# K's parameters loaded and worked in two halves, table loads as steps of the order, two late tiles by way of a ring, and a new order of steps

## The chip, the cores and the metric

The kernel runs on one core of a Trainium2 chip. The core's engines run side by side, each through its own queue in program order: TensorE (PE, with its weight loads PEld), VectorE (DVE), ScalarE (ACT), GpSimd (POOL) and the queue of SyncE (SP), which issues nearly all DMAs. The metric is the device time of one execution in microseconds; lower is better. A span is the time from the first to the last instruction in the trace.

## The reference

The input u is 2048 x 640 (length by channels), nearly everything is bf16. Two branches read it and a gate mixes them:

```python
g  = sigmoid((u * gate_w).sum(-1))                      # one number a row
# branch a: a long convolution with a kernel K of a diagonal state space
dt = exp(log_dt); logdA = dt * (A_re + 1j*A_im); dB = dt * (B_re + 1j*B_im)
K  = einsum("dn,dnl,dn->dl", C_re + 1j*C_im, exp(logdA[:, :, None] * l), dB).real   # 640 x 2048, n = 128
a  = irfft(rfft(u, 4096) * rfft(K, 4096))[:2048] + u * Dskip
# branch b: a gated feed forward, F = 1728
b  = (gelu(u @ w_gate) * (u @ w_up)) @ w_down
out = g * a + (1 - g) * b
```

## The kernel before

**One order, written by hand.** The function builds a dictionary of small named steps; the text ORDER (lines 40 to 89) lists their names, and the loop at lines 829 to 834 issues them one after the other. The order in the text is the program order of every engine: an engine takes its own steps out of it in that order, and waits where a semaphore for data or for a buffer isn't there yet. A name is followed by `/0` to `/3` where the step opens one of the four PSUM tiles `PS` (each 128 x 2 x 512), and by `/A` or `/D` where a copy may be done by ACT or DVE.

**K's parameters.** `lp0` to `lp5` (line 265) load A_re, A_im, C_re, C_im, B_re, B_im as six pieces of 128 x 640 (160 KB each), lp0 on ACT's queue, the others on SP's. `t0` to `t5` (`turn`, line 297) bring the 128 states onto the partitions: ten matmuls of 128 x 64 each. From these, steps `dt`, `al`, `al2`, `th`, `c2`, `c3`, `v0` to `v18`, `mag`, `at` and `ph45` (lines 317 to 350 and 560) work out the decay, the angle, the size and the phase of every (state, channel) on 128 x 640 tiles, each in one instruction of DVE or ACT.

**Tables of K, by halves h of the channels (320 each).** K at a lag is a product of a coarse and a fine power. `tables(h)` fills two tables: exponentials on ACT (`xb`, `xa`, lines 447 to 461), then phases on DVE (`fb`, `fa`, lines 469 and 477, each ended by a quarter-turn copy `ph_q`, line 464), sines on ACT (`sb`, `sa`, lines 481 and 487), and products on DVE (`pb`, `pc`, `pa`, `ma`, lines 492 to 505). `ct` (lines 517 and 518) contracts them over the states on PE, `ek` unloads PSUM (two or four casts of 128 x 504), `kd` and `kt` regroup the result through DRAM into KTt. The tables of the second half overwrite those of the first after its seven `ct`.

**ACT's function tables** are loaded by five steps with places of their own: `tabE` (exponential and logarithm), `tabT` (sine and arctangent), `tabE2`, `tabT2`, `tabG` (gelu and tanh), lines 316, 548, 558 and 617.

**Feed forward.** `g` and `u` steps (line 376) are gate and up projections of 128 columns each, for both halves of the rows (`.0`, `.1`): ten matmuls of 128 x 512 a step. Weights come in pairs into two slots (`lw0` to `lw13`), x by DMA transposes (`x0.0` to `x4.1`). The results are cast out of PSUM (`eg`, `eu`) into H or, through a ring of three tiles, to DRAM (`sg`, `su` into Gd and Ud), and come back later (`rg`, `rl`); `ge` is the gelu on ACT, `hm` the product on DVE. The tile H1 lies over the table space, so it is free only after the second contraction. The four tiles LATE = 8 to 11 of the second half of the rows are worked last and go straight into H1: `dg` (line 425) the gelu from PSUM, `du` (line 433) the product.

**Convolution.** In the spectrum: u is folded (`ul`, `ur`, `uf`, `us`) and turned by constant matrices FM (`U`, line 693), K by KMa and KMb (`K`, line 706); DVE multiplies the pieces (`m`, `s`, `y`, lines 748 to 755), IM turns back (`I`, line 766), and `D` (line 781) adds the down projection, `Z` (lines 788 and 789) mixes both branches with the gate in PSUM; `o` scales and `st` stores. `eU`, `eK`, `eI` copy out of PSUM. Names carry channel half, block of 512 rows and piece; the products of block 3 of half 1 end with `y130` and `y131`, followed by I130, I131, Z130, D131 and Z131. FM, KMa, KMb and IM are constants of the program and are loaded whole by `lfm`, `lkm`, `lkm2`, `lim` on SP's queue (lines 599 to 605).

Of the kernel before, what the change touches and what calls it, by code (L numbers as in the profile page):

```python
# [11 lines left out]
ALU = mybir.AluOpType  # L12
# [6 lines left out]
TURN = 65536.0  # L19
# [14 lines left out]
VIA = ()  # L34
# [6 lines left out]
ldt leu2 lp3 one oa.0 idx sk ob.0 lp0 lpk tdt/0 t0/1 tabE dt al xb27.0 al2 xa4.0 xb14.0 xb17.0 xb4.0 xb8.0 xa1.0  # L41
xb23.0 lp2 lw0 lp1 x0.0 lp5 x3.0 lp4 x1.0 x2.0 t1/2 th fb1.0 fb0.0 x4.0 t5/3 t2/0 xb2.0 c2 t3/1 c3 v3 v2 xa11.0 xb6.0
xa10.0 xa14.0 t4/2 v0 v1 v4 xa5.0 xb29.0 xb11.0 xb25.0 v6 v5 v7 v8 v11 g0.0/0 xb10.0 xa3.0 v9 v10 eg0.0/D v12 g1.0/1
v13 eg1.0/D xa8.0 xb9.0 xb5.0 xb1.0 xa7.0 xb19.0 v14 v15 xa19.0 xa15.0 xa17.0 xb15.0 xb13.0 xa9.0 v16 xb31.0 xb7.0
xa16.0 xb21.0 xb3.0 xb12.0 tabT sb0.0 u0.0/3 x3.1 leu0 ul0 lw1 ur0 uf0.1 eu0.0/D u1.0/2 g2.0/0 uf0.0 v17 mag ma2.0
u2.0/1 eu2.0/A ma4.0 eg2.0/D v18 su0.0 lw2 fil.0 ma6.0 ma1.0 eu1.0/D ur1 ma0.0 ma3.0 u3.0/3 fb2.0 pb0.0 pc0.0 sb1.0
fb3.0 eu3.0/A pb1.0 pc1.0 su1.0 lsk ul1 g4.0/0 g3.0/2 lw3 eg4.0/A sb2.0 pb2.0 fb4.0 pc2.0 eg3.0/A at ph45 su3.0 su2.0
us0 u5.0/1 u4.0/3 g5.0/0 lw4 sb3.0 pb3.0 pc3.0 fb5.0 eu4.0/A eu5.0/A sb4.0 g7.0/2 g6.0/3 eg6.0/A eg5.0/A u6.0/1 sb5.0
eg7.0/A pb4.0 pc4.0 fa0.0 pb5.0 fa1.0 sa0.0 su5.0 eu6.0/A u8.0/3 u7.0/0 lgw su4.0 x1.1 x2.1 lu00 x0.1 lw5 g8.0/2 su6.0
sa1.0 eg8.0/A g9.0/1 fa2.0 pa0.0 sa2.0 eu7.0/A uf1.0 uf1.1 pa1.0 u9.0/2 eg9.0/A eu8.0/A eu9.0/A fa4.0 pa2.0 fa3.0  # L50
sa4.0 g11.0/0 eg11.0/A sa3.0 lw6 g12.0/1 eg12.0/A su8.0 su9.0 x4.1 us1 su7.0 pa4.0 fa6.0 leu1 ul2 sa6.0 pa3.0 fa5.0
g10.0/3 eg10.0/A sa5.0 pa6.0 ma5.0 pa5.0 u11.0/2 eu11.0/A u10.0/0 u12.0/1 ur2 eu10.0/A ct0.2/3 ct0.1/2 ct0.4/0
eu12.0/A ek0.4/A fb0.1 uf2.0 ek0.2/D uf2.1 ct0.0/1 ct0.6/3 ek0.6/D ek0.1/A ct0.3/0 ct0.5/2 ek0.3/D ek0.0/D ek0.5/D
ks.0 lw7 su10.0 su11.0 h.0/3 eg13.0/D ul3 su12.0 us2 ob.1 ur3 tabE2 xa11.1 xb11.1 xb3.1 xb21.1 xa17.1 xb19.1 xa9.1
xa15.1 xa16.1 eu13.0/D uf3.0 ma5.1 lw8 h.1/0 oa.1 xa7.1 xb23.1 g12.1/1 xa3.1 xa14.1 xa10.1 ma3.1 eg12.1/D xb5.1 xb27.1
xb1.1 xb17.1 xa19.1 xb14.1 xb10.1 xb13.1 xb4.1 xb7.1 xb31.1 xb25.1 xb9.1 xa8.1 xb6.1 xb12.1 xb2.1 xb8.1 xa4.1 xb29.1
xa1.1 xa5.1 xb15.1 tabT2 sb0.1 u12.1/2 eu12.1/D su13.0 eg13.1/D sg13.1 sg12.1 leu3 su12.1 uf3.1 ma2.1 u0.1/3 eu0.1/D
ma6.1 g0.1/1 g1.1/2 kd.0 lw9 eu13.1/A gl/3 gl1 ma4.1 fb1.1 ma1.1 eg0.1/D sg0.1 su0.1 lfm ma0.1 us3 sb1.1 u1.1/1 g2.1/0
lw10 su13.1 fb2.1 pb0.1 pc0.1 pb1.1 pc1.1 sb2.1 U000/3 eg2.1/A eU000/A fb4.1 pb2.1 pc2.1 eg1.1/A eu1.1/A fb3.1 fil.1
sb4.1 sg2.1 u2.1/0 sg1.1 eu2.1/A su1.1 lkm fa0.1 pb4.1 pc4.1 sb3.1 g3.1/3 U001/2 eU001/A u3.1/1 eg3.1/A u4.1/0 U003/2  # L60
# [24 lines left out]
st110 D111/2 Z111 o111/A U131/0 eU131/A D120/3 m1210 s1220 m1211 m1221 s1221 m1200 s1200 m1201 s1201 m1320 m1310 s1320
y120 y121 m1311 m1321 s1321 m1330 s1330 m1331 K133/1 K131/2 eK131/A s1331 eK133/A m1300 s1300 m1301 s1301 y131 I121/0
# [53 lines left out]
def kernel(  # L140
# [724 lines left out]
```

## Time and profile before

| | |
|---|---|
| median of 3 runs | 290.28 us (289.33 to 291.79) |
| profiled execution | 288.91 us |
| its span | 287.1 us |
| PE busy | 264.5 us (92%) |
| DVE busy | 261.8 us (91%) |
| ACT busy | 222.7 us (78%) |
| DMA | 46.94 MB, mean 163 GB/s |
| granted TensorE clock, mean | 0.988 |

The page of the profile gives busy times of each engine and a picture of the span in 40 slices. Windows give the same for stretches that one chooses. The view of waits lists for each engine what ended its idle time: engine and line that waited, then who was waited for, the sum in us, how often, the longest. In groups and timelines a row is: line of the kernel, engine, operation, what is written and read, shapes, count; the groups then show the busy time and the mean length in ns of one, the timelines begin with start and length in us. The length of one instruction includes some overlap with the next of its engine.

### The profile page before, as it was taken

How to read it: one execution, taken by the hardware profiler on the slowest of the kernel's cores; microseconds unless marked ns; L12 is line 12 of the kernel's file. 1: busy time of each engine (PE TensorE's matmuls, PEld its weight loads, DVE VectorE, ACT ScalarE, POOL GpSimd, SP SyncE). 2: the span in 40 equal slices, each digit the busy share in tenths (PEclk: the TensorE clock that was granted, in tenths of full speed). 3: DMA queues.
4: the chain of work that ended last, by engine and by line, in shares of the span. 5: the costliest groups of instructions: out<-in, count | busy, mean ns of one | idle time of the engine just before them, and what ended most of it. 6: DMA issues, size and time to landing. Idle time of an engine off the chain costs nothing.

```text
span 287.1 us, 4933 instructions
## 1 busy us (share of the span) xinstructions
PE 264.5 (92%) x1883; PEld 159.8 (56%) x1883; DVE 261.8 (91%) x336; ACT 222.7 (78%) x324; POOL 14.1 (5%) x23
## 2 busy tenths in 40 slices
PE   3899799999999699998799998999999999999974
PEld 1744344444754434444584455777777767777753
DVE  1689999999998898999999999999999999999960
ACT  4699999799899978999999988999856545313320
POOL 2202000030040000000010000000000000000000
PEclk9999999999999969999999999999999999999999
DMA  7992479979382897858948877782355000010001
GB/s 200 221 227 75 136 223 272 213 182 304 101 265 66 193 321 220 301 186 263 332 117 222 278 200 215 225 256 67 95 142 162 25 23 23 25 46 25 23 23 46
DMA packets 63148, 46.94 MB, mean 163 GB/s; under 512 B 23275, under 2 KB 53526, under 8 KB 62998
## 3 DMA queue, kind: packets, MB, share of 16 engines
q1 hardware_dynamic: 62166, 44.90, 55.4%
q0 software_dynamic: 384, 1.31, 1.6%
q10 hardware_dynamic: 576, 0.43, 0.5%
q8 instruction: 14, 0.23, 0.3%
q14 instruction: 8, 0.07, 0.1%
HBM read 29.39 MB, written 14.62 MB: 153 GB/s over the span
## 4 chain that ended last, share of the span: by engine, by line
PE 36%; DVE 32%; ACT 17%; DMA 8%; issue 4%; SPq 2%; POOL 0%; DVEq 0%; ACTq 0%
PE ps L376 15%; DVE work L751 8%; DVE work L752 8%; PE ps L781 7%; DVE work L748 5%; PE ps L693 4%; ACT tail L481 3%; DMA work<-PMd 3%; PE ps L766 2%; ACT work L381 2%; ACT tail L487 2%; PE ps L706 2%; DVE work L383 2%; PE ps L517 2%; DMA tail<-PMd 2%
## 5 line engine op out<-in xcount | busy, mean ns | idle before, releaser
L376 PE MATMUL ps<-xT,Wr 128*128 128x512 bf16 x540 | 122.1, 385 | 7.1 <-DVE work L383 3.2
L376 PEld LDWEIGHTS <-Wr 128*128 128x128 bf16 x540 | 53.3, 99 | 72.4 <-issue 12.5
L381 ACT CAST work<-ps 128x640 bf16<-128x640 f32 (+2 forms) x59 | 47.8, 842 | 14.2 <-PE ps L766 7.5
L387 ACT ACTIVATE Wr<-ps,gs 128x320 bf16<-128x320 f32 x29 | 13.7, 524 | 29.4 <-issue 16.4
L752 DVE TENSOR_TENSOR work<-work 128x2560 bf16<-128x2560 bf16 x24 | 35.8, 1490 | 0.7
L781 PE MATMUL ps<-xT,work 128*128 128x320 bf16 x224 | 31.7, 299 | 0.0
L781 PE MATMUL ps<-xT,H 128*128 128x320 bf16 x224 | 31.6, 299 | 0.0
L481 ACT ACTIVATE tail<-work 128x1920 bf16<-128x1920 int16 x14 | 25.7, 1854 | 1.8 <-DVE work L464 1.7
L781 PEld LDWEIGHTS <-H 128*128 128x128 bf16 x224 | 21.9, 98 | 8.5
L781 PEld LDWEIGHTS <-work 128*128 128x128 bf16 x224 | 21.9, 98 | 8.5
L505 DVE TENSOR_TENSOR work<-tail,work 128x1920 bf16<-128x1920 bf16 (+1 forms) x22 | 23.1, 1090 | 0.0
L487 ACT ACTIVATE tail<-work 128x960 bf16<-128x960 int16 (+1 forms) x24 | 20.8, 926 | 0.8 <-DVE work L505 0.8
L766 PE MATMUL ps<-work,tail 128*128 128x320 bf16 x128 | 19.5, 299 | 1.8 <-DVE work L754 1.8
L469 DVE SCALAR_TENSOR_TENSOR work<-tail 128x320 int32<-128x320 f32 x42 | 18.0, 483 | 0.9 <-ACT tail L487 0.5
L464 DVE TENSOR_SCALAR work<-work 128x960 int32<-128x960 int16 (+1 forms) x26 | 16.5, 634 | 1.3
L766 PEld LDWEIGHTS <-tail 128*128 128x128 bf16 x128 | 12.4, 98 | 7.4 <-issue 2.2
L693 PEld LDWEIGHTS <-early 128*128 128x128 bf16 x128 | 12.4, 98 | 7.1 <-DMA tail<-PMd 1.7
L706 PE MATMUL ps<-KTt,early 128*128 128x320 bf16 x80 | 15.0, 299 | 1.4 <-ACT early L387 1.2
L496 DVE TENSOR_TENSOR work<-tail,work 128x1920 bf16<-128x1920 bf16 x14 | 15.9, 1151 | 0.3 <-ACT tail L481 0.3
L383 DVE CAST work<-ps 128x1024 bf16<-128x1024 f32 (+2 forms) x11 | 12.4, 1146 | 2.6 <-PE ps L766 1.6
L457 ACT ACTIVATE work<-tail 128x320 bf16<-128x320 f32 x30 | 12.5, 454 | 1.4 <-DVE tail L319 1.4
L693 PE MATMUL ps<-work,early 128*128 128x320 bf16 x80 | 13.1, 299 | 0.0
(119 smaller groups left out, 405.6 us busy)
## 6 DMA issues: line engine op xcount, KB each, us to landing
Ud<-work SPq DMA_DIRECT2D x22, 256.0 KB
work<-Ud SPq DMA_DIRECT2D x22, 256.0 KB
Wr<-in_B_w_gate_dram SPq DMA_DIRECT2D x12, 320.0 KB
Wr<-in_B_w_up_dram SPq DMA_DIRECT2D x12, 320.0 KB
PMd<-early SPq DMA_DIRECT2D x4, 640.0 KB
Gd<-work SPq DMA_DIRECT2D x9, 256.0 KB
work<-Gd SPq DMA_DIRECT2D x9, 256.0 KB
out_dram<-Wr SPq DMA_DIRECT2D x14, 160.0 KB
```

Of the source, the lines that this page charges most:

```text
L376: P.matmul(t[:, x, :], lhsT=Wr[:, slot, kt, cols:cols + 128], rhs=xT[:, th, kt, 512 * x:512 * x + 512], start=(kt == 0), stop=(kt == 4))
L381: A.copy(out=out, in_=in_)
L383: V.tensor_copy(out=out, in_=in_)
L481: act(out=T, in_=low16(t)[:, :, :, ::2], func=ACT.Sin, scale=SIN_SCALE)
L487: act(out=o[:, r], in_=i[:, r], func=ACT.Sin, scale=SIN_SCALE)
L505: tt(out=B2[:, :, :, cols].rearrange("p r g x -> p g r x"), in0=Tv if hf == 0 else Tv[:, :, ::-1], in1=e, op=ALU.mult)
L693: P.matmul(t[:, r, 0:W2], lhsT=FM[:, e, r, 128 * m:128 * m + 128], rhs=pm[:, r, e], start=(e == 0), stop=(e == 1))
L706: P.matmul(t[:, r, 0:W2], lhsT=mat[:, r, 128 * m:128 * m + 128], rhs=KTt[:, q, d], start=(x == 0 and j != 1), stop=(x == len(seq) - 1), sk ...
L751: step(f"m{h}{c}{i}{part}", lambda ux=ux, kx=kx: tt(out=fl(t), in0=ux, in1=kx, op=ALU.mult))
L752: step(f"s{h}{c}{i}{part}", lambda dst=dst, op=op: tt(out=fl(dst), in0=fl(dst), in1=fl(t), op=op))
L766: P.matmul(t[:, r, 0:W2], lhsT=IM[:, m, r, 128 * e:128 * e + 128], rhs=Y[:, r, m], start=(m == 0), stop=(m == 3))
L781: P.matmul(t[:, x, 0:W2], lhsT=H[c // 2][:, ft, tk:tk + 128], rhs=at[f"Wd{h}"][:, ft], start=(ft == 0), stop=False)
```

## The change

- The six parameters come as twelve pieces of 64 partitions: `lp0.0` to `lp5.1`, all but lp0.0 on SP. Each turn is done for one half of the channels (`t0.0` to `t5.1`, five matmuls of 64 rows), and every step from `al` to `ph45` exists for each half on 128 x 320. `dt` stays whole.
- Words `tE`, `tT` and `tG` in ORDER load a function table at that place; there are nine of them instead of five loads. The first stands ahead of ACT's own two loads.
- The quarter-turn copy of the phases is a step of its own (`qa`, `qb`).
- FM, KMa, KMb and IM are laid out by pieces and loaded in 4, 4, 2 and 2 parts.
- VIA = (8, 9): of the four late tiles, two are worked in the ring, stored to Gd and loaded into H1 again (`sg8.1`, `sg9.1`, `rg8.1`, `rg9.1`).
- ORDER is new throughout, with some copies given to another engine. From ACT to DVE: eK000, eK012, eU002, eU003, eU013, eg1.1, eg3.0, ek0.1, ek0.4, ek1.1, ek1.2, eu13.1, eu2.1, o1300, o1301, o1311. From DVE to ACT: eI131, eK011, eK013, eU010, eg1.0, eg13.0, eg7.1, ek1.5, eu13.0.

The diff, cut to its core (of ORDER, its beginning and its end):

```diff
-VIA = ()
+VIA = (8, 9)
...
-ldt leu2 lp3 one oa.0 idx sk ob.0 lp0 lpk tdt/0 t0/1 tabE dt al xb27.0 al2 xa4.0 xb14.0 xb17.0 xb4.0 xb8.0 xa1.0
-xb23.0 lp2 lw0 lp1 x0.0 lp5 x3.0 lp4 x1.0 x2.0 t1/2 th fb1.0 fb0.0 x4.0 t5/3 t2/0 xb2.0 c2 t3/1 c3 v3 v2 xa11.0 xb6.0
...
-y130 I120/2 D121/1 eI120/A Z120 o120/A eI121/A D130/2 Z121 o121/D I130/3 I131/0 eI130/A Z130 eI131/D D131/1 Z131 st111
-st120 st121 o1300/A st1300 o1310/D o1301/A st1301 st1310 o1311/A st1311
+tE oa.0 ob.0 one idx lpk lp0.0 lp1.1 ldt tdt/0 t0.0/1 dt al.0 xa10.0 lp5.1 lp4.0 lp2.0 lp3.0 xb19.0 al2.0 xa5.0 xa11.0
+lw0 lp1.0 xb13.0 t3.0/2 c3.0 xa7.0 xb3.0 xa16.0 xb8.0 xa15.0 x1.0 lp5.0 t2.0/3 x0.0 lp2.1 x2.0 lp3.1 c2.0 xb29.0
+xb14.0 xb17.0 t1.0/0 th.0 fb0.0 fb1.0 xb15.0 t5.1/1 t4.0/2 t5.0/0 v2.0 v1.0 v0.0 v4.0 v3.0 v5.0 v6.0 v7.0 v8.0 qb1.0
+xb11.0 v11.0 lp0.1 x4.0 x3.0 lp4.1 t3.1/3 t2.1/2 xa1.0 c2.1 qb0.0 c3.1 v2.1 v3.1 ur0 t0.1/0 t1.1/2 ul0 v9.0 v10.0
+t4.1/3 v12.0 v13.0 tT sb0.0 sb1.0 v0.1 v1.1 mag.0 v4.1 v5.1 tE v6.1 v7.1 v14.0 v15.0 xb21.0 xb7.0 u0.0/1 eu0.0/D
...
+s1321 m1330 s1330 m1331 s1331 K131/3 K130/1 eK131/A eK130/A m1300 s1300 m1301 s1301 eI111/A D101/0 D110/3 Z110 st100
+D111/1 Z111 o111/A y130 y131 Z101 I120/2 D120/1 o101/A eI120/A Z120 st101 o120/A o110/A D121/0 I121/2 eI121/A D130/1
+Z121 I130/3 I131/2 eI130/A Z130 eI131/A D131/3 Z131 st110 o121/D st111 o1300/D o1301/D st120 st121 o1310/D o1311/D
+st1300 st1301 st1310 st1311
...
+    kinds = {"tE": "natural_log_exp_and_others", "tT": "trig_and_small", "tG": "gelu_apprx_tanh_and_others"}
...
-    for i in range(6):
-        step(f"lp{i}", lambda i=i: (A if i == 0 else S).dma_start(out=at["prm"][:, i],
-                                                                 in_=PRM[i].rearrange("(p j) n -> p (j n)", p=128)))
+    def load_p(i, h):
+        rows = PRM[i].rearrange("(p j) n -> p (j n)", p=128)
+        (A if i + h == 0 else S).dma_start(out=at["prm"][64 * h:64 * h + 64, i], in_=rows[64 * h:64 * h + 64])
...
-    def turn(i):
-        t = PS[bank[f"t{i}"]]
-        for h in range(2):
-            o = t[:, h, 0:W2].rearrange("p (g j w) -> p j w g", g=16, w=4)
-            for j in range(5):
-                P.matmul(o[:, j], lhsT=at["prm"][:, i, 128 * j:128 * j + 128], rhs=ident[:, 64 * h:64 * h + 64],
-                         start=True, stop=True)
+    def turn(i, h):
+        o = PS[bank[f"t{i}.{h}"]][:, 0, 0:W2].rearrange("p (g j w) -> p j w g", g=16, w=4)
+        q = slice(64 * h, 64 * h + 64)
+        for j in range(5):
+            P.matmul(o[:, j], lhsT=at["prm"][q, i, 128 * j:128 * j + 128], rhs=ident[q, q], start=True, stop=True)
...
-    step("al", lambda: tt(out=two(at["al"][:, 0]), in0=pv(0), in1=two(at["dtb"]), op=ALU.mult))
+    def params(h):
+        d = slice(W2 * h, W2 * h + W2)
+        dtb, al, th, mag, ph45 = at["dtb"][:, d], at["al"][:, :, d], at["th"][:, d], at["mag"][:, d], at["ph45"][:, d]
+        va, vb, vr, vi, sm = (at[x][:, d] for x in ("va", "vb", "vr", "vi", "sm"))
...
+        s_("al", lambda: tt(out=al[:, 0], in0=pv(0), in1=dtb, op=ALU.mult))
...
-                    step(f"dg{ft}", lambda j=j, ft=ft: act(out=halves(H[1][:, ft]), in_=PS[bank[j]][:], func=ACT.Gelu_apprx_tanh))
+                    dst = ring() if ft in VIA else H[1][:, ft]
+                    step(f"dg{ft}", lambda j=j, dst=dst: act(out=halves(dst), in_=PS[bank[j]][:], func=ACT.Gelu_apprx_tanh))
...
+                    if ft in VIA:
+                        step(f"sg{ft}.1", lambda dst=dst, ft=ft: S.dma_start(out=Gd[:, ft], in_=dst))
...
-        ph_q(t, 3)
...
+                step(f"qa{c}.{h}", lambda t=t: ph_q(t, 3))
...
-    step("lfm", lambda: S.dma_start(out=at["FM"], in_=FMd))
+    for m in range(4):
+        step(f"lfm{m}", lambda m=m: load_part("FM", FMd, m, 512))
...
+    for ft in VIA:
+        step(f"rg{ft}.1", lambda ft=ft: S.dma_start(out=H[1][:, ft], in_=Gd[:, ft]))
...
         for word in ORDER.split():
             name, _, how = word.partition("/")
+            if name in kinds:
+                A.preload_act_table_set(kinds[name])
+                continue
```

More of the change, by code (lines that the diff above doesn't have):

```diff
@@ L56 @@
[L56 to L60, printed above, removed]
@@ L340 @@
-    step("v9", lambda: act(out=va, in_=va, func=ACT.Ln))
-    step("v10", lambda: act(out=sm, in_=va, func=ACT.Exp, scale=0.5))
-    step("v11", lambda: ts(out=vb, in0=vr, scalar1=0.0, scalar2=2.0, op0=ALU.is_ge, op1=ALU.mult))
-    step("v12", lambda: stt(out=sm, in0=vb, scalar=-1.0, in1=sm, op0=ALU.add, op1=ALU.mult))
-    step("v13", lambda: tt(out=vb, in0=vr, in1=sm, op=ALU.add))
-    step("v14", lambda: act(out=va, in_=vb, func=ACT.Square))
-    step("v15", lambda: act(out=va, in_=va, func=ACT.Ln))
@@ L353 @@
+    for h in range(2):
+        params(h)
     step("idx", lambda: G.iota(back[:], pattern=[[512, 4], [-128, 2]], base=255, channel_multiplier=-1))
@@ L603 @@
     step("hz1", lambda: G.memset(H[1][64:128, 13], 0.0))
-    step("lkm2", lambda: S.dma_start(out=at["KMb"], in_=KMd[:, 4096:6144]))
-    step("lim", lambda: S.dma_start(out=at["IM"], in_=IMd))
+    for m in range(2):
+        step(f"lkb{m}", lambda m=m: load_part("KMb", KBd, m, 1024))
+    for e in range(2):
+        step(f"lim{e}", lambda e=e: load_part("IM", IMd, e, 1024))
     def gate_mm():
```

198 lines of the change are left out of this document (106 added, 92 removed).

## The prediction

> **What bounds the kernel now.** I read the page first (who is busy, and when), then the windows that split the span into stages, then the waits of DVE, then the timelines of both ends, and last the groups by shape, for prices.
>
> ```profile
> span 287.1 us, 4933 instructions
> PE 264.5 (92%) x1883; PEld 159.8 (56%) x1883; DVE 261.8 (91%) x336; ACT 222.7 (78%) x324; POOL 14.1 (5%) x23
> DVE  1689999999998898999999999999999999999960
> PE 36%; DVE 32%; ACT 17%; DMA 8%; issue 4%; SPq 2%; POOL 0%; DVEq 0%; ACTq 0%
> ```
>
> Two engines are over 90% busy, and the chain passes from one to the other, so no single share names the bound. The windows do (columns: PE, PEld, DVE, ACT, POOL busy, granted clock, DMA):
>
> ```profile
> 0.00:20.00 20.00, 13.74 (x89) 8.98 (x90) 10.99 (x20) 13.94 (x26) 3.96 (x11) 1.00 0.98 228
> 100.00:120.00 20.00, 18.58 (x79) 8.28 (x79) 18.99 (x32) 17.50 (x21) 0.00 (x0) 0.85 0.93 289
> 120.00:140.00 20.00, 18.38 (x95) 9.09 (x94) 19.43 (x34) 20.00 (x20) 0.00 (x0) 1.00 0.79 240
> 180.00:276.00 96.00, 94.36 (x691) 67.30 (x690) 94.28 (x80) 54.58 (x96) 0.00 (x0) 1.00 0.28 83
> 276.00:287.10 11.10, 7.22 (x52) 4.98 (x51) 2.39 (x5) 2.16 (x4) 0.00 (x0) 0.99 0.14 44
> ```
>
> DVE is short of full only in the first 20 us and in the last 11. Its waits say the same:
>
> ```profile
> DVE tail L319 <- PE ps L297: 5.0, 1, 5.0
> DVE Wr L389 <- PE ps L789: 4.0, 1, 4.0
> DVE tail L322 <- PE ps L297: 3.0, 1, 3.0
> DVE work L383 <- PE ps L766: 1.6, 1, 1.6
> DVE work L383 <- DMA Gd<-work: 0.9, 1, 0.9
> DVE early L367 <- DMA early<-in_A_u_dram,back: 0.9, 1, 0.9
> DVE work L339 <- ACT work L338: 0.8, 1, 0.8
> DVE work L469 <- ACT tail L487: 0.5, 1, 0.5
> DVE early L383 <- PE ps L518: 0.4, 1, 0.4
> ...
> ```
>
> L319 and L322 lie in the first 10 us, L389 and the L383 behind L766 in the last 11. What is left, the five in between, is 0.9 + 0.9 + 0.8 + 0.5 + 0.4 = 3.5 us; the rows below them are 0.3 or less each. So between 10 and 276 us DVE has nearly nothing to wait for: its end is its start plus its work. And the end of the kernel hangs on it:
>
> ```profile
> 275.28 0.82 DVE L754 TENSOR_TENSOR work<-work 128x1280 bf16<-128x1280 bf16 x1
> 276.15 2.33 PE L766 MATMUL ps<-work,tail 128*128 128x320 bf16 x16 [1.77 <-DVE work L754]
> 278.86 3.97 PE L781 MATMUL ps<-xT,work 128*128 128x320 bf16 x28
> 283.41 0.55 DVE L389 TENSOR_SCALAR Wr<-ps,gs 128x320 bf16<-128x320 f32 x1 [4.00 <-PE ps L789]
> ```
>
> After the last product (y130 here) come two inverses, one more down projection, scaling and store: 287.1 - 276.1 = 11 us. In the new order y131 is last, and behind it PE has the same I130, I131, Z130, D131, Z131; I keep the 11 us. So I ask of each edit what it does to DVE ahead of that product.
>
> **Copies that change engine.** I compared the engine letters of both orders. Gate and up copies go four each way (eg3.0, eg1.1, eu2.1, eu13.1 to DVE; eg1.0, eg7.1, eg13.0, eu13.0 to ACT), those of K's spectrum two each way: nothing. Of the unloads of the contraction, four go to DVE (ek0.1, ek0.4, ek1.1, ek1.2) and one leaves (ek1.5): three more, two casts each. Of U's spectrum three go (eU002, eU003, eU013) and one leaves (eU010): two more. The three outputs that go to DVE at the very end lie in its idle time there, and eI131 leaves it: nothing.
>
> ```profile
> L383 DVE CAST early<-ps 128x504 bf16<-128x504 f32 x9 | 5.6, 674 | 0.5 <-PE ps L518 0.4
> L383 DVE CAST work<-ps 128x640 bf16<-128x640 f32 x2 | 1.6, 824 | 1.6 <-PE ps L766 1.6
> L344 DVE TENSOR_TENSOR work<-work 128x640 f32<-128x640 f32 x1 | 0.8, 824 | 0.0
> L469 DVE SCALAR_TENSOR_TENSOR work<-tail 128x320 int32<-128x320 f32 x42 | 18.0, 483 | 0.9 <-ACT tail L487 0.5 <-ACT tail L481 0.3
> L320 DVE TENSOR_SCALAR tail<-tail 128x640 f32<-128x640 f32 x1 | 0.5, 493 | 0.0
> L477 DVE TENSOR_SCALAR work<-tail 128x320 int32<-128x320 f32 x32 | 8.5, 318 | 0.0
> ```
>
> Six casts of 5.6/9 = 0.62 us are 3.7 us, two of 1.6/2 = 0.8 are 1.6: together 5.3 us more on DVE, and as much less on ACT, which has room (222.7 of 287.1).
>
> **Parameters by halves.** The same elements in twice the instructions. Fourteen DVE operations of 640 columns become 28 of 320, three that only scale become six. In a row of such operations one starts 0.74 us after the other:
>
> ```profile
> 13.05 0.81 DVE L334 TENSOR_TENSOR work<-ps,early 128x640 f32<-128x640 f32 x1
> 13.79 0.81 DVE L333 TENSOR_TENSOR work<-ps,early 128x640 f32<-128x640 f32 x1
> ```
>
> Half of one is nearest to L469: 18.0/42 = 0.43 us in a row, 0.48 alone. A split costs 2 x 0.43 - 0.74 = 0.12 to 2 x 0.48 - 0.82 = 0.14 us, fourteen times 1.7 to 2.0; for the scaling ones 2 x 0.27 - 0.49 = 0.05, three times 0.15. I take 1.8. That the phase and its quarter-turn copy become two steps changes no instruction. DVE's sum is 5.3 + 1.8 = 7.1 us, 6.4 if the copies run into one another as closely as the 0.74 shows for 0.82; I take 6.7, between them.
>
> **The start.** SP issues the loads of the parameters one by one, between the transposes of x:
>
> ```profile
> 6.02 0.57 SPq L265 DMA_DIRECT2D early<-in_A_B_im_dram  x1
> 8.05 0.58 SPq L265 DMA_DIRECT2D early<-in_A_B_re_dram  x1
> 8.68 5.45 SPq L280 DMA_TRANSPOSE xT<-in_A_u_dram  x4
> DMA to landing us min/median/max: 4.2/4.3/4.5
> 8.11 5.81 PE L297 MATMUL ps<-picks,early 128*128 128x64 bf16 x50 [3.20 <-DMA early<-in_A_A_im_dram]
> 13.67 1.13 PE L376 MATMUL ps<-xT,Wr 128*128 128x512 bf16 x4
> ```
>
> Five loads on SP become eleven; at about 0.45 us each SP is done 6 x 0.45 = 2.7 us later, at 16 to 16.5 instead of 14.1, and the last issue is lp4.1. Landing takes 4.3 us, so t4.1 can't run before 20, and every gate matmul stands behind it on PE: gate work starts at about 20.5 instead of 13.67. DVE has the first half's chain to work on meanwhile. Counted from th.0 (whose load lp1.0 again follows a pair of weight loads, so again at 9.4 to 9.7), it has two phases, six products, v8, two quarter turns, v11, two products of the other half, v12 and v13. That is some 8 us by the 0.43 and 0.27 above, with about 0.5 of waiting for the squares (0.8 at L339 today, where they are twice as long), so it stands at v0.1 at about 18.3: 2 us ahead of t4.1. Bounds 0 (the halves land sooner than whole loads) and +2.5; I take +0.8, nearer to the lower end, since what lands is half the bytes of that row. On ACT's queue the table load now stands ahead of the loads of picks and A_re:
>
> ```profile
> 0.75 0.38 ACTq L265 DMA_DIRECT2D early<-in_A_A_re_dram  x1
> 1.64 1.28 ACT L316 ACT_TABLE_LOAD   x1 [1.64 <-PEq L849]
> 79.61 1.28 ACT L548 ACT_TABLE_LOAD   x1
> 80.90 0.47 ACT L447 ACTIVATE work<-tail 128x320 bf16<-128x320 f32 x1
> ```
>
> That may put al.0 off by up to 1.3 us; th.0 waits for its own load anyhow (the 3.0 us of L322 covers it), so nothing; without that cover 1.3.
>
> **Tables of ACT.** Five loads become nine: 4 x 1.28 = 5.1 us, and some ten half activations more at 0.1 each. ACT gives up about what DVE takes over, and ends near its old sum; it has 2.5 us idle between 100 and 120, none between 120 and 140. The next activation starts at 80.90, right at the load's end. The Trainium skill, ScalarE: Activation LUTs, section What ACT_TABLE_LOAD costs, counts 1283 ns and a drain of 1380 ns for every switch, and its section on table sets says to do all of one set before the next, which speaks against this edit; by it the four would be an estimated 10.6 us. The trace shows the 1283 ns and no drain.
>
> **The rest.** FM, KMa, KMb and IM come in 12 pieces instead of 4, and two late tiles go out and come back: 12 more issues on SP at no more than the 0.58 above, spread over 100 us. The ring tiles let four of the late gate matmuls run ahead of the second contraction, so PE, not DVE, gains there. The cover is that loads are issued ahead of their use; where it is gone, a load is late by one issue, 0.6 us. I put all this at 0, bounds -1 and +1.5.
>
> **The sum.** Of the 3.5 us of waits in between, the new order can at most take all; some come back elsewhere, since ACT has no idle left at 120 to 140. I take 2.8 off. 6.7 + 0.8 - 2.8 = +4.7: span 291.8. The profiled execution took 288.91 (1.8 beside its span), the median of the runs is 290.28; with the same 4.7 the median is 295.0. Own range of this case: 6.4 + 0 - 3.5 - 1 = +1.9 to 7.1 + 2.5 - 2.0 = +7.6, so 292.2 to 297.9.
>
> **Rivals.** *Halves start DVE earlier.* A half is half the bytes. If th.0's load lands 2.0 us earlier and t4.1's in time, the 3.0 of L322 falls to 1.0, all 3.5 go, and 287.1 + 6.4 - 2.0 - 3.5 = 288.0 in the span, 291.2 as a median: not slower by the bound below. Over 1% faster needs another 3.8 us, from L319's wait and the tail. For: the two longest waits stand exactly there. Against: the DMA engines have 0.98 of busy share in these 20 us, and lp1.0 is queued behind the weights. It decides from L322's wait below 1.5 us. Chance 0.30.
>
> *PE takes over.* Its gates start 6.8 us later, and its remaining work is the same; in 180 to 276 it is busy for 94.36 of 96 us. If its stalls of today stay (20 - 18.58 and 20 - 18.38 in two windows alone), it ends 6.8 later and makes DVE wait for banks besides: 287.1 + 6.8 + 2 = 295.9, a median of 299. Against: the ring tiles fill two of these stalls. Chance 0.17.
>
> *Switching of tables stalls ACT for as long again as the load row shows,* as the drain of the page named above would. Two of the four added loads fall among the second half's tables, and there, from 100 to 140 us, ACT is busy for 37.5 of 40, so 2 x 1.28 go to DVE's waits: 291.8 + 2.6 = 294.4, a median of 297.6. The row at 80.90 speaks against it. Chance 0.03.
>
> **The numbers.** A measurement of this kernel tells about 1% (2.9 us) from no change. Forecast 0.50: mostly above 293.2, 0.42 slower and 0.08 same. Early halves 0.30: 0.20 same, and 0.10 faster, which stands for a start or a tail that I misread. PE and tables 0.20, slower. Together faster 0.10, same 0.28, slower 0.62. The range reaches from 288, three below the early-halves case, to 299.5, just over PE's.
>
> **What would show it.** DVE's busy time 268 to 270 instead of 261.8 (the three outputs included); the casts of 128x504 on DVE up by six, of 128x640 without a factor three of U's; first gate matmul at 19 to 21; nine table loads of 1.28; the last product at 280 to 282 and 11 us behind it. It is wrong if DVE is not busier by 6 us, if its first 20 us hold clearly more than 11 us of work, or if less than 10 us follow the last product.

## The result

The kernel after takes 294.37 us (median of 4 runs, 293.3 to 294.68), the kernel before 290.76 us on the same chip (4 runs, 289.33 to 291.79): 3.6 us more. The recorded ratio is 1.0134, 95% interval 1.0104 to 1.0163 (the quotient of the two medians is 1.0124). The forecast was 295.0. The profiled execution took 294.4 us with a span of 292.4, 5.3 more than before. The execution of the kernel before that was profiled, 288.91 us, is faster than each of these four, so some 1.7 us of what the two traces show between the kernels is chance between executions. From the page of the kernel after:

```profile
span 292.4 us, 4995 instructions
PE 264.8 (91%) x1870; PEld 158.5 (54%) x1883; DVE 264.9 (91%) x363; ACT 223.9 (77%) x328; POOL 28.1 (10%) x23
DVE  1587999999999999979997999899999999999971
DVE 43%; PE 17%; issue 14%; DMA 12%; ACT 9%; SPq 3%; DVEq 0%; ACTq 0%
```

DVE is busier by 3.1 us, not by 6 to 8, and PE's share of the chain fell from 36% to 17%. To see where the time went I cut both spans at three events that both kernels have: the first matmul of the first contraction, the end of the second half's last table product, and the end of the last spectrum product. Windows of before, then of after (columns as in the prediction: length, then PE, PEld, DVE, ACT, POOL busy, granted clock, DMA):

```profile
0.00:74.65 74.65, 65.27 (x322) 31.86 (x323) 64.52 (x104) 66.72 (x89) 8.93 (x15) 1.00 0.78 200
74.65:141.78 67.13, 61.36 (x487) 32.78 (x487) 62.92 (x102) 63.16 (x88) 3.59 (x5) 0.95 0.76 227
141.78:276.10 134.32, 130.70 (x1023) 90.15 (x1022) 132.03 (x130) 90.62 (x145) 1.61 (x3) 1.00 0.41 121
276.10:287.10 11.00, 7.22 (x52) 4.98 (x51) 2.29 (x4) 2.16 (x4) 0.00 (x0) 0.99 0.15 45
```

```profile
0.00:80.54 80.54, 68.57 (x326) 32.42 (x333) 67.13 (x126) 71.39 (x102) 24.57 (x17) 1.00 0.73 196
80.54:146.33 65.79, 61.16 (x483) 32.35 (x490) 64.03 (x109) 63.37 (x83) 1.37 (x3) 1.00 0.80 230
146.33:281.56 135.23, 128.40 (x1014) 89.13 (x1014) 130.84 (x125) 87.80 (x143) 2.14 (x3) 1.00 0.43 123
281.56:292.40 10.84, 6.70 (x49) 4.59 (x47) 2.94 (x7) 1.38 (x2) 0.00 (x0) 1.00 0.15 46
```

| stage | length | DVE busy | DVE idle (length less busy) | ACT busy |
|---|---|---|---|---|
| 1, to the first contraction | +5.89 | +2.61 | 10.13 to 13.41, +3.28 | +4.67 |
| 2, to the last table product | -1.34 | +1.11 | 4.21 to 1.76, -2.45 | +0.21 |
| 3, to the last spectrum product | +0.91 | -1.19 | 2.29 to 4.39, +2.10 | -2.82 |
| behind it | -0.16 | | | |

The loss is in stage 1, and ACT's work grows there more than DVE's; which of them carries the stage is told further below. DVE's waits after:

```profile
DVE tail L340 <- ACT early L322: 5.3, 1, 5.3
DVE tail L343 <- PE ps L310: 4.3, 1, 4.3
DVE Wr L413 <- issue: 3.4, 1, 3.4
DVE H L710 <- DMA work<-Ud: 3.1, 4, 1.6
DVE work L407 <- PE ps L400: 2.2, 1, 2.2
DVE Wr L413 <- PE ps L817: 1.5, 1, 1.5
DVE work L495 <- ACT tail L505: 1.4, 1, 1.4
```

The first two and the L407 are the start (the angle of the first half, and the first cast of a projection), the two L413 the end. Of the five waits of before between 10 and 276 us only the one for the squares is left, with 0.5; in their place stand `hm` products that wait for their tile to come back through the ring (L710), and a phase that waits for sines (L495).

### The profile page after: what moved, and what is told of

It reads as the page before. It is cut to its first block, busy times and chain, and to the rows that moved or that the text cites. A ratio compares the mean times of both kernels' runs of the same rounds, so it can differ in the third digit from the quotient of the medians.

```text
span 292.4 us, 4995 instructions
## 1 busy us (share of the span) xinstructions
PE 264.8 (91%) x1870; PEld 158.5 (54%) x1883; DVE 264.9 (91%) x363; ACT 223.9 (77%) x328; POOL 28.1 (10%) x23
## 4 chain that ended last, share of the span: by engine, by line
DVE 43%; PE 17%; issue 14%; DMA 12%; ACT 9%; SPq 3%; DVEq 0%; ACTq 0%
PE ps L809 7%; DVE work L779 5%; DVE work L529 5%; DVE work L780 5%; DMA Wr<-in_B_w_gate_dram 4%; PE ps L794 4%; ACT work L405 3%; DVE work L776 3%; DVE work L495 3%; DMA work<-Ud 3%; DVE work L407 3%; PE ps L400 2%; DVE work L490 2%; DVE early L391 2%; DVE H L710 2%
## 5 line engine op out<-in xcount | busy, mean ns | idle before, releaser
L400 PE MATMUL ps<-xT,Wr 128*128 128x512 bf16 x527 | 120.2, 384 | 4.0 <-DMA Wr<-in_B_w_gate_dram 1.5
L411 ACT ACTIVATE Wr<-ps,gs 128x320 bf16<-128x320 f32 x26 | 12.1, 527 | 22.4 <-issue 15.5
L384 POOL DMA_INDIRECT early<-in_A_u_dram,back x8 | 22.8, 2851 | 53.0 <-DVE early L391 37.0
L495 DVE SCALAR_TENSOR_TENSOR work<-tail 128x320 int32<-128x320 f32 x42 | 18.0, 481 | 1.4 <-ACT tail L505 1.4
L721 PE MATMUL ps<-work,early 128*128 128x320 bf16 x80 | 13.9, 299 | 2.4 <-ACT work L405 0.8
L407 DVE CAST work<-ps 128x1024 bf16<-128x1024 f32 (+2 forms) x11 | 12.8, 1178 | 2.3 <-PE ps L400 2.2
```

Of the source, the lines that this page charges most:

```text
L384: G.indirect_dma_start(out=at["ur"][:, e, :], out_offset=None, in_=u2[:, :], in_offset=bass.IndirectOffsetOnAxis(ap=back[:, 2 * c + e:2 * ...
L400: P.matmul(t[:, x, :], lhsT=Wr[:, slot, kt, cols:cols + 128], rhs=xT[:, th, kt, 512 * x:512 * x + 512], start=(kt == 0), stop=(kt == 4))
L407: V.tensor_copy(out=out, in_=in_)
L495: stt(out=t[:, 0, x], in0=at["th"][:, d], scalar=float(A_OF[3 * c + x] + MID), in1=at["ph45"][:, d], op0=ALU.mult, op1=ALU.add)
L721: P.matmul(t[:, r, 0:W2], lhsT=FM[:, m, e, r], rhs=pm[:, r, e], start=(e == 0), stop=(e == 1))
```

## Experiments

All times are medians; each ratio is to the kernel before, run beside it on the same chip. Differences to the kernel after are taken between sessions, in which the median of the kernel before lay between 289.77 and 290.76 us, so a difference of 1 us is not clear by itself.

**The quarter turn.** The prediction costed its separate step at nothing. Two runs ask that: the step added to the kernel before, and taken from the kernel after.

```diff
-        ph_q(t, n)
+                step(f"qb{c}.{h}", lambda t=t, n=n: ph_q(t, n))
...
-... fb2.0 pb0.0 pc0.0 sb1.0
+... fb2.0 pb0.0 qb2.0 pc0.0 sb1.0
```

> The kernel before, with the quarter-turn copies as steps of their own, one DVE step behind their phase; nothing else is changed, no instruction added. Theory (the quarter turn, which the prediction costed at nothing, is what DVE gained): a DVE instruction that reads what the one right ahead of it wrote starts about 0.03 us after that one's end, one that doesn't starts about 0.08 before it; 19 of the 26 pairs are taken apart, 19 x 0.11 = 2.1 us, so about 288.7 instead of 290.8, and DVE's busy time falls by about 1.5. Rival (the placing of the copy costs nothing, and the work that DVE lacked after the change went elsewhere): no change within 0.5 us.

293.26 us, ratio 1.008 (1.0047 to 1.0113): slower by about 1%. DVE's busy time fell, from 261.8 to 260.7 (1.5 was said), but stage 2 grew by 2.9 us. Each sine on ACT now starts one DVE step later, and DVE waits for it in turn:

```profile
DVE work L471 <- ACT tail L487: 2.3, 1, 2.3
DVE work L471 <- ACT tail L481: 1.5, 2, 1.1
DVE work L496 <- ACT tail L481: 1.1, 4, 0.3
```

In the kernel before these three pairs of engines cost 0.5, 0.3 and 0.3. Neither the theory nor the rival held: the copy's place is worth DVE time, and it is also the place from which ACT is fed.

```diff
-                step(f"qa{c}.{h}", lambda t=t: ph_q(t, 3))
+        ph_q(t, 3)
...
-... pc3.0 fa0.0 qb5.0 qa0.0 pc4.0 ...
+... pc3.0 fa0.0 pc4.0 ...
```

> The kernel after, with every quarter-turn copy right behind its phase again, as before; nothing else. Theory (the 26 dependent pairs cost 0.11 us each): +2.5 to +2.9 us, about 297, with DVE's busy time up by about 2. Rival: no change within 0.5 us.

296.36 us, ratio 1.0196 (1.0155 to 1.0236), 2.0 us above the kernel after; the two intervals overlap a little. DVE's busy time is 267.1 instead of 264.9, and 1.73 of these 2.2 us stand in stage 1, which is 2.23 us longer with the same work on ACT (this run's row of it, against 67.13 of DVE and 71.39 of ACT in 80.54):

```profile
0.00:82.77 82.77, 69.07 (x332) 32.47 (x333) 68.86 (x127) 71.48 (x102) 14.31 (x17) 1.00 0.74 196
```

The theory holds in DVE's work; in the whole time it is short, 2.0 us for 2.5 to 2.9. In the order after, with room for the later sines, the separate step is worth 2.2 us of DVE.

**The copies.** Nine engine letters, moved alone in either direction.

```diff
-... ek0.4/A ... ek0.1/A ... eU003/A ... eU002/A ... ek1.5/D ... ek1.1/A ek1.2/A ... eU013/A ... eU010/D
+... ek0.4/D ... ek0.1/D ... eU003/D ... eU002/D ... ek1.5/A ... ek1.1/D ek1.2/D ... eU013/D ... eU010/A
```

> The kernel before, with nine letters of the kernel after and nothing else: ek0.1, ek0.4, ek1.1, ek1.2, eU002, eU003, eU013 to DVE, ek1.5 and eU010 to ACT. Theory (DVE's work carries the end): six more casts of 128x504 at 0.62 and two more of 128x640 at 0.8 are 5.3 us more of DVE and the time grows by 4 to 5.3 us, to 295 to 296. Rival (DVE waits for ACT in these stretches, where ACT has no idle time): what ACT is relieved of comes back as shorter waits, and the time grows by less than 2 us.

> The kernel after, with the same nine letters set back to those of before. Theory (DVE's work carries the end): 4 to 5.3 us less, 289 to 290. Rival (after the change ACT carries nine table loads and the half activations, and is full from 100 to 146 us): DVE waits there for ACT instead, and the time stays within 1 us of 294.4 or grows.

Before with the letters of after: 306.0 us, ratio 1.0545 (1.0489 to 1.0601). After with the letters of before: 302.55, ratio 1.0417 (1.0379 to 1.0455), 8.2 above the kernel after. Both are worse: the first by far more than theory or rival allowed, the second on the side of its rival, which had put no size to it. Stage 2 of both, in the same order:

```profile
74.61:155.83 81.22, 66.64 (x488) 35.80 (x488) 66.85 (x108) 60.93 (x83) 3.59 (x5) 0.89 0.63 193
```

```profile
80.35:149.10 68.75, 62.82 (x489) 32.91 (x490) 61.56 (x103) 66.61 (x89) 1.03 (x3) 0.98 0.76 220
```

In the first, DVE is busier by 3.9 us and idle for 14.4 us instead of 4.2. It stands for 3.0 us at an unload of the contraction and for 5.1 at a copy of K's spectrum, with all its later work behind it, and PE waits for DVE in turn (3.85 us in the contraction, 3.70 ahead of a projection). In the second DVE has 2.5 us less to do and is idle for 7.2 instead of 1.8: ACT is at 66.61 of 68.75. That makes 3.0 us of loss; the other 5.2 lie in stage 3 (140.45 against 135.23 us), where one of the unloads set back to ACT now stands behind two gelus and PE waits for it:

```profile
160.94 1.76 PE L734 MATMUL ps<-KTt,early 128*128 128x320 bf16 x6 [4.92 <-ACT tail L405]
```

So the letters are not a term by themselves. Two readings are left, and no run separates them. One is that the copies are the other half of the table loads: ACT takes loads, DVE takes copies, and either half alone loses. The other is that an order written for one assignment loses with any other, whatever the loads. Stage 3 of the kernel after holds no table load, so its 5.2 us speak for the second.

**The table loads.**

```diff
-sb3.1 g2.1/0 ...
+tG tT sb3.1 g2.1/0 ...
...
-... eU001/A sa2.1 ...
+... eU001/A tG tT sa2.1 ...
```

> The kernel after with four more loads of ACT's function tables, as two pairs in the second half's tables (gelu's and back, ahead of sb3.1 and ahead of sa2.1), 4 x 1.28 = 5.1 us of ACT between 110 and 140 us. The prediction put the four loads that the change adds at nothing, because ACT has room over the whole span. If that holds: +1 us at most. Rival (in this stretch ACT is busy for 37.6 of 40 us and DVE's products wait for its sines): the loads come through one for one, +4 to +5.1 us, 298.5 to 299.5. Second rival (each load holds ACT for as long again): +8 to +10 us, and a gap of over 1 us behind each load.

300.64 us, ratio 1.0337 (1.0283 to 1.039): 6.3 us above the kernel after, for 5.1 us of loads. In the profiled execution stage 2 takes 72.99 instead of 65.79 us, and stage 1 is the same within 0.1. "Nothing" was wrong for loads in this stretch; the first rival (4 to 5.1) is nearest. ACT's timeline shows no second stall behind a load, 108.89 + 2.57 = 111.46:

```profile
108.89 2.57 ACT L860 ACT_TABLE_LOAD   x2
111.47 1.90 ACT L511 ACTIVATE tail<-work 128x960 bf16<-128x960 int16 x2
```

That speaks, as in the prediction, against the drain of 1380 ns that the Trainium skill, ScalarE: Activation LUTs, section What ACT_TABLE_LOAD costs, counts with every switch. What may make them cost more than their length is told under the clock, below.

**Working by halves.** The parameters of the kernel before worked, not loaded, by halves in place.

```diff
-... tabE dt al xb27.0 al2 xa4.0 ...
+... tabE dt al.0 al.1 xb27.0 al2.0 al2.1 xa4.0 ...
```

> The kernel before with the parameters worked, but not loaded or turned, by halves at the same places: 17 operations of DVE and 9 of ACT on 128x640 become two each on 128x320. The prediction's term is +1.8 us of DVE work (14 x 0.12 to 0.14 and 3 x 0.05) and as much in the time, 292.1. Rival (a half step can start while the other half is still on the other engine, so waits between ACT and DVE shorten): 0. Third case (each half waits for the one before it, and ACT's nine splits delay its exponentials): +3 or more.

290.24 us, ratio 1.0004 (0.9985 to 1.0022): nothing, the number of the first rival. Its reason, shorter waits, is not seen: DVE is idle for 25.4 us of the span, against 25.3. DVE's busy time grew by 0.7 us (262.5). The kernel after shows why it isn't 1.8. Half products with nothing between them start 0.40 apart, not 0.43, and 2 x 0.40 - 0.74 = 0.06; fourteen of these are 0.8:

```profile
12.35 0.48 DVE L352 TENSOR_TENSOR work<-ps,early 128x320 f32<-128x320 f32 x1
12.75 0.48 DVE L351 TENSOR_TENSOR work<-ps,early 128x320 f32<-128x320 f32 x1
```

**The start.** Two tries at taking back stage 1's loss in the kernel after, and one at the wait for the angle alone, in the kernel before.

```diff
-... lp0.0 lp1.1 ldt tdt/0 t0.0/1 dt al.0 xa10.0 lp5.1 lp4.0 lp2.0 lp3.0 xb19.0 al2.0 xa5.0 xa11.0
+... lp0.0 lp1.0 ldt tdt/0 t0.0/1 dt al.0 xa10.0 lp2.0 lp3.0 lp4.0 lp5.0 xb19.0 al2.0 t1.0/0 th.0
...
+... u0.0/2 v13.0 mag.0 v14.0 v15.0 xb17.0 xb15.0 eu0.0/D t3.1/0 c3.1 t2.1/1 c2.1 t5.1/3 t4.1/0 v2.1 ...
```

> The kernel after with its first 40 us in another order, the same steps: all first halves of the parameters are loaded first, then the first weights and x, then the second halves; the phase step fb0 and the first sines come before the squares of the size; the first two projections stand ahead of most turns of the second half; the later phases fb2 and fb3 stand ahead of the first cast. Theory (the start is what the change loses: its first contraction comes 5.9 us later than before, 74.65 against 80.5 us, and DVE waits for 12.3 of the first 40 us): the waits of 4.3 us (angle) and 2.2 us (first cast) go, the first gate matmul comes at 14 to 16 us, and the time falls by 3 to 5 us, to 290 to 291. Rival (ACT, with its exponentials and table loads, or the load of u, is as late as before): DVE waits for ACT before 40 us instead and the time changes by less than 1.5 us.

311.35 us, ratio 1.0767 (1.0707 to 1.0827). The angle came at 6.11 us and the first gate matmul at 11.56, earlier than the theory's 14 to 16, and then PE and DVE ran dry, the first row on PE, the second on DVE:

```profile
33.16 11.11 PE L400 MATMUL ps<-xT,Wr 128*128 128x512 bf16 x43 [5.70 <-DMA Wr<-in_B_w_up_dram]
```

```profile
39.13 1.23 DVE L407 CAST H<-ps 128x1024 bf16<-128x1024 f32 x1 [8.35 <-PE ps L400]
```

The second weight pair stood on SP behind `ur0`, which waits until all turns have read the parameters that it overwrites. The next run puts the weights ahead of it (its edit against this run).

```diff
-... lp1.1 lp4.1 xa15.0 ... ur0 ul0 xb21.0 ... lw1 eu1.0/D u2.0/2
+... lp0.1 lp1.1 lw1 fb2.0 tE ... t1.1/2 ur0 ul0 al.1 th.1 ... eu1.0/D u2.0/1
```

> The start of the experiment before, mended where its trace shows the loss: the second weight pair is loaded ahead of ur0 and ul0 (those two wait on SP for the turns, and the weights stood behind them until 33 us), the turns of the second half run in one go behind the first projection, and ACT's two copies c3.1 and c2.1 stand ahead of its late exponentials. Theory (the start is what the change loses, and a microsecond gained by DVE ahead of the first contraction reaches the end): no wait of 8 us at 39, first contraction at 76 to 78 instead of 80.5, time 290 to 292. Rival (the first 80 us are bound by ACT, whose exponentials and sines are the same sum, 76.8 of the 80 us from 20 to 100 us being busy): DVE's early lead is lost in waits for ACT before the first contraction, and the time stays at 293 to 296.

303.7 us, ratio 1.0487 (1.043 to 1.0545). Neither the theory nor the rival: that wait is gone, and the next queue shows (DVE, then PE):

```profile
DVE early L391 <- DMA early<-in_A_u_dram,back: 6.1, 1, 6.1
```

```profile
45.77 14.60 PE L400 MATMUL ps<-xT,Wr 128*128 128x512 bf16 x56 [8.76 <-ACT H L405]
```

The first folds of u came 2.6 us later than in the kernel after (27.32 against 24.77), and the next one waits for its load. Both runs lose behind 20 us what they gain ahead of it; neither says what the kernel after's start would be worth if it could be had alone.

```diff
-ldt leu2 lp3 ... al2 xa4.0 ... lp2 lw0 lp1 x0.0 ... x2.0 t1/2 th fb1.0 fb0.0 ...
+ldt leu2 lp1 ... al2 t1/2 th fb1.0 fb0.0 xa4.0 ... lp2 lw0 lp3 x0.0 ...
```

> The kernel before with one pair of loads exchanged on SP, whole parameters as before: lp1 (the angle) is issued first and lp3 in its place, behind the first weights; its turn, the angle and the first two phases stand right behind al2, and ACT's copies c2 and c3 some exponentials earlier. It puts the wait of L322 by itself: 3.0 us before the change, 4.3 after it. Theory (DVE's end is its start plus its work): the angle comes at 6.4 to 6.6 instead of 9.39, the first cast at 17.8 instead of 19.6, and 1.5 to 3 us reach the end, 287.5 to 289. Rival (ACT, busy for 19.9 of the 20 us from 20 to 40, or PE's first projection sets the pace there): DVE waits for them instead, 0 to -0.5 us.

289.69 us, ratio 0.9979 (0.9955 to 1.0003): the rival. In its trace the angle stands 3.1 us earlier, the first contraction 0.43 us, the end nowhere:

```profile
6.30 0.81 DVE L322 SCALAR_TENSOR_TENSOR tail<-ps,early 128x640 f32<-128x640 f32 x1
11.90 0.82 DVE L334 TENSOR_TENSOR work<-ps,early 128x640 f32<-128x640 f32 x1 [1.86 <-ACT early L326]
19.42 1.22 DVE L383 CAST H<-ps 128x1024 bf16<-128x1024 f32 x1 [0.47 <-PE ps L376]
```

1.86 of it go at once to a wait for ACT's copy of C, 0.47 to PE's first projection. In the kernel before, a wait of DVE in the first 20 us is not paid one for one: ACT and PE set the pace there.

**The waits for the ring.**

```diff
-hm1.0 K000/3 ... rl4.0 ... eK000/D ks.1 ...
+K000/3 ... rl4.0 ... eK000/D ks.1 hm1.0 ...
...
-hm13.0 ... rl2.1 m0210
+... rl2.1 m0210 hm13.0
```

> The kernel after with two products of the feed forward moved: hm1.0, which waits 1.6 us for its tile from the ring, behind eK000 and ks.1; hm13.0, which waits 0.74, behind m0210. Theory (DVE's waits in the middle add to the end one for one): 1.5 to 2.3 us less, 292 to 293. Rival (PE, which is 93 to 100 per cent busy from 180 us on, ends no earlier, or the ring is freed later and the wait comes back at the next product): no change within 0.7 us.

306.94 us, ratio 1.0582 (1.0546 to 1.0617). This measures something else than it was meant to. `rl4.0` and `rl2.1` fill the same ring tiles as the two products that I moved behind them, so those products work on tiles 4 and 2, and must wait for them: DVE waits 14.7 us for two loads. The next run moves these loads too; in it, D000 of the down projection still reads tile 13 of H ahead of its product.

```diff
-hm1.0 ... rl4.0 ... ks.1
+... ks.1 hm1.0 rl4.0
...
-hm13.0 ... D000/2 ... rl2.1 m0210
+... D000/2 ... m0210 hm13.0 rl2.1
```

> The kernel after with hm1.0 behind eK000 and ks.1, and hm13.0 behind m0210, each with the one load that fills its ring tile next behind it (rl4.0, rl2.1), so that every product reads its own tile again. Theory (DVE's waits in the middle add to the end one for one): of 1.6 and 0.74 us of waiting 1.5 to 2.3 go, 292 to 293. Rival (PE is 93 to 100 per cent busy from 180 us on, or the loads moved back bring the wait again at hm4.0): no change within 0.7 us.

294.39 us, ratio 1.015 (1.01 to 1.0199): unchanged. Here the product must wait until D000 has read its tile, and what the other product had gained goes there:

```profile
184.95 0.68 DVE L710 TENSOR_TENSOR H<-H,work 64x1024 bf16<-64x1024 bf16 x1 [2.44 <-PE ps L809]
```

So one product alone:

```diff
-hm1.0 ... rl4.0 ... ks.1
+... ks.1 hm1.0 rl4.0
```

> The kernel after with the one product hm1.0, which waits 1.60 us for its tile, behind eK000 and ks.1, and the load rl4.0 that fills its tile next behind it. Theory (a wait of DVE in the middle adds to the end one for one): the first product of the spectrum starts 1.5 to 1.8 us earlier, as it did in the last experiment (158.33 against 160.14), and 1 to 1.8 us reach the end, 292.6 to 293.4. Rival (the lead of 1.8 us is lost behind 180 us, where PE is over 93 per cent busy and DVE waited 2.4 us for PE in that experiment): no change within 0.5 us.

293.25 us, ratio 1.0104 (1.0076 to 1.0133): 1.1 us less than the kernel after, as the theory has it at its lower end, though the intervals overlap. In the trace stage 3 is shorter by 0.84 us, and the waits for the ring fell from 3.1 to 2.2 us:

```profile
146.20:280.59 134.39, 128.56 (x1014) 89.20 (x1014) 130.82 (x126) 87.70 (x143) 2.14 (x3) 1.00 0.43 123
```

The way of the two late tiles through the ring was not undone by itself, but the trace of the kernel after shows what it does to the loads. SP stores the two tiles (L460), and the next load into the ring (L709) stands for 2.6 us until such a store has landed; the load that `hm1.0` waits for is issued 1.0 us behind it, at 153.56 (SP's timeline, then its waits from 146 to 156 us):

```profile
148.09 1.45 SPq L460 DMA_DIRECT2D Gd<-work  x2
152.56 0.32 SPq L709 DMA_DIRECT2D work<-Ud  x1
```

```profile
SPq L709 <- DMA Gd<-work: 2.6, 1, 2.6
```

No version beat both kernels; the fastest, the earlier angle, can't be told from the kernel before.

## Why the prediction was right, and where it was not

**The form of the sum** held. The last product ends at 281.56 (280 to 282 was said), 10.84 us follow it (11), the first gate matmul starts at 19.14 (19 to 21), there are nine table loads of 1.28, and the first 20 us hold 9.71 us of DVE's work (at most 11). Up to the last product the sum was 6.7 + 0.8 - 2.8 = 4.7; measured, in the stages above, it is 2.53 of work + 3.28 of start - 0.35 of other waits = 5.46. Two large errors of opposite sign made a good total; that is luck. The medians moved by 3.6 us for the 4.7 that was forecast.

**DVE's work, 6.7: measured 2.53**, and by the prediction's own line ("wrong if DVE is not busier by 6 us") its account of the work was wrong, though the time came out. Three steps of it failed. "Changes no instruction", of the quarter turn: worth 2.2 us of DVE. Halves at 1.8: 0.7. Copies at 5.3: 5.0 by the letters added to the kernel before (261.8 to 266.7), 3.3 by those taken from the kernel after (264.9 to 261.6). With 3.3 to 5.0, 0.7 and -2.2 the sum is 1.8 to 3.5, and the 2.53 lies in it.

**Copies as a cost and table loads at nothing** was a further error. The prediction read ACT's room from the whole span (222.7 of 287.1). By stage there is next to none: 66.72 of 74.65 us and 63.16 of 67.13. It named the full stretch from 100 to 140 itself, and used it only for a rival at 0.03. Four further loads in that stretch cost 6.3 us for 5.1, and the copies, set back, cost 8.2 us where the prediction's term has a gain. That the copies pay for the loads is one reading of this; the runs do not show it. The rival *switching of tables* was wrong in its mechanism (no drain), right in where it looked.

**The start, 0.8: measured 3.28 of DVE's idle time.** The wait that it priced, for t4.1 not before 20 us, did not come: lp4.1 was issued at 15.38 (the working's 14.1 + 2.7 would put SP's end at 16.8, not 16 to 16.5), its turn ran at 18.50, sooner than with the 4.3 us of landing, and DVE worked v0.1 at 19.32 without waiting. What it priced at nothing came: the angle at 10.41 and not at 9.4 to 9.7, and 2.2 us at the first cast; the bound of +2.5 was too narrow. What such a wait is worth depends on the engine that carries the stage. The chain of stage 1 by line, before, then after (the view cuts its lines off):

```profile
by line: PE ps L376 20.7%; ACT tail L481 9.6%; ACT tail L487 8.9%; ACT work L381 6.4%; ACT H L381 6.1%; DMA early<-in_A_B_im_dram 4.6%; PE ps L297 4.5%; ACT work L457 4.5%; ACT work L449 4.3%; ACT work L461 4.3%; issue 4.0%; ACT work L447 3
by line: DVE work L529 12.7%; DVE work L495 10.6%; issue 8.6%; DVE work L490 6.9%; DVE early L391 5.7%; DVE work L520 5.4%; PE ps L400 5.2%; DMA early<-in_A_A_im_dram 5.1%; DVE work L516 4.9%; DVE work L502 4.4%; DVE H L407 4.2%; SPq L276 3
```

Summed by engine it is ACT 42.6, PE 18.8 and DVE 1.2 us of 74.65 before, and DVE 53.8, PE 6.3 and ACT 4.1 of 80.54 after. The chain is one path, and another may be hardly shorter, but the runs agree with it. In the kernel before, 3.1 us less waiting of DVE moved the first contraction by 0.43, and 0.7 us more work of the halves moved nothing. In the kernel after, 1.73 us more work of DVE (the fused quarter turns) made stage 1 longer by 2.23. So the prediction's picture, that DVE's end is its start plus its work, was wrong in stage 1 of the kernel before, where it was read, and fits the kernel after. The 5.89 of stage 1 are there 2.61 of DVE's work and 3.28 of its idle time. Of the 2.61, some 1.6 are two folds of u (0.82 each) that the new order moved from stage 2 to stage 1. No run removed the 3.28 without losing elsewhere.

ACT has 4.67 us more work in stage 1, of which two more table loads are 2.57 (groups of ACT in stage 1 of the kernel after):

```profile
L860 ACT ACT_TABLE_LOAD x4 | 5.1, 1283 | 0.8 <-PEq L880 0.7
L364 ACT ACTIVATE work<-work 128x320 f32<-128x320 f32 x2 | 0.9, 464 | 2.2 <-DVE work L363 2.2
L345 ACT CAST early<-ps 128x320 bf16<-128x320 f32 x2 | 0.8, 405 | 0.0
```

and the 16 half activations and 4 half copies of the parameters, of which two rows stand here, are about 1.8 (16 x 0.46 + 4 x 0.41 = 9.0, against 7.2 for the ten whole ones of the kernel before). In the chain of that stage ACT stands for 4.1 us only; no run took its two loads out of it, so what they cost there stays open.

**The waits, -2.8: measured -0.35.** The range had 2.0 to 3.5 off, so this lies outside it. Stage 2 gave 2.45, near the 2.8. Stage 3 took 2.10 back, by the step that put two tiles' way through the ring and 12 more issues at 0 because "loads are issued ahead of their use". They were late by up to 1.6 us, behind the 2.6 us that SP stood for the stores of the late tiles; undoing the longest of these waits gave 1.1.

**The rivals.** *Halves start DVE earlier* hung on L322's wait falling below 1.5; it grew from 3.0 to 4.3. With the angle that early in the kernel before, 0.4 us came of it. *PE takes over*: its gates start 5.5 us later, but its idle time up to the last product grew only from 18.8 to 23.4 us (length less busy, stages 1 to 3), and the chain left it.

## What to carry to other kernels

Read an engine's room in the stage where the work goes, not from its share of the span: 22% of idle time in ACT over the span were 11 and 6% in the two stages that got the loads. Where two engines are full in turn, price an exchange between them as one edit together with its order: the copies alone, in the old order, cost some 16 us, the new order without them 12 (the kernel before took 290.25 beside both), and both together 3.6. What a wait is worth depends on the engine that carries the stage behind it: 3.1 us of DVE ahead of the first contraction were worth 0.4 at it in the kernel before, where ACT and PE carry that stage, while 1.6 in the last stage were worth 1.1.

## What was not expected of the hardware

A PE that stands still for 2 to 3 us may pay again. In the kernel before, 80 one-column matmuls in 2.14 us and a wait of 2.09 come ahead of this row, and 20 matmuls take 6.97 us where the next 20 take 4.48 (timeline of PE, then a window):

```profile
100.86 6.97 PE L376 MATMUL ps<-xT,Wr 128*128 128x512 bf16 x20 [2.09 <-DVE work L383]
108.93 4.48 PE L376 MATMUL ps<-xT,Wr 128*128 128x512 bf16 x20 [0.56 <-ACT work L381]
```

```profile
100.00:104.00 4.00, 3.14 (x8) 1.16 (x8) 3.89 (x8) 3.95 (x6) 0.00 (x0) 0.50 1.11 314
```

The granted clock of these 4 us is 0.50.

In the run with more table loads a wait of 3.18 us did the same:

```profile
114.32 6.03 PE L400 MATMUL ps<-xT,Wr 128*128 128x512 bf16 x14 [3.18 <-ACT work L405]
```

14 matmuls at 4.48/20 = 0.224 are 3.1 us, so this wait cost 2.9 us more than its length. A second stretch follows two waits of 1.14 and 1.90 us, with ten matmuls in 4.47 instead of 2.2 us. The granted clock of both is 0.50 (timeline, then the windows of both):

```profile
142.60 4.47 PE L400 MATMUL ps<-xT,Wr 128*128 128x512 bf16 x10
```

```profile
113.28:120.11 6.83, 5.79 (x14) 2.02 (x14) 6.67 (x9) 6.80 (x9) 0.00 (x0) 0.50 0.50 151
140.59:147.41 6.82, 5.83 (x17) 2.37 (x17) 6.47 (x12) 6.76 (x7) 0.00 (x0) 0.50 0.64 187
```

PE lost some 5 us by this, more than the 1.2 by which 6.3 exceeds the 5.1 us of loads. That the clock is what made 6.3 of 5.1 is argued, and so is its part in the cost of the letters (clock 0.89 in that stage 2). In the kernel after, a wait of 1.54 us had no such effect, and the 0.85 of the kernel before is gone:

```profile
125.23 2.33 PE L400 MATMUL ps<-xT,Wr 128*128 128x512 bf16 x10 [1.54 <-DMA Wr<-in_B_w_gate_dram]
```

The Trainium skill, TensorE: Matmul & The Clock Gate, Part 1, says that the array's clock is halved after an idle window of about 3.4 us and released after as long a busy one. These rows agree in kind, and the two stretches above last 6.8 us each. The waits are shorter than that window: 3.18 us, and 2.09 behind 2.14 us of one-column matmuls, so matmuls of one column seem to count as idle; no run tests them alone.

The second is on DVE. The half products above are 0.48 us long and start 0.40 apart: the second starts before the first has ended. A quarter turn that reads what the phase right ahead of it wrote starts 0.03 behind that one's end (from the run with the earlier angle, 7.15 + 0.80 = 7.95):

```profile
7.15 0.80 DVE L477 TENSOR_SCALAR work<-tail 128x320 int32<-128x320 f32 x3
7.98 0.66 DVE L464 TENSOR_SCALAR work<-work 128x960 int32<-128x960 int16 x1
```

That is 0.11 us a pair. In the order after, 21 of the 26 pairs stand apart (not all 26, as the expectation has it), 21 x 0.11 = 2.3, near the 2.0 us by which putting them together again made the time longer. Of the 0.11, 0.03 is idle time, so the busy time should grow by 21 x 0.08 = 1.7; it grew by 2.2, and the rest is not explained.
